# Block 1's layer norm statistics ahead of the last two angle tables, and the loads of x for blocks 2 and 3 behind block 0's state DMAs

## The chip, the cores and the metric

The kernel runs on one core of a Trainium2 chip. The metric is the device time of one execution in microseconds (us), the median of several runs. One further execution is taken by the hardware profiler; the times of single instructions come from that one.

The engines have these names in the profile: PE is TensorE, PEld its weight loads, DVE is VectorE, ACT is ScalarE, POOL is GpSimd, and SP is SyncE, which here only issues DMAs. DMAs issued by SP and ACT run on queue q1, those issued by POOL on queue q0.

## The reference

The input x has 2048 tokens of 512 channels. It is normalized (mean and variance per token, no gain), and the result xn goes through two branches that are added to x.

```python
xn = _layernorm(x)
# branch A: a diagonal state space layer
Lam_bar = exp(dt * Lam)                       # 512 complex poles
Bu = einsum("bld,pd->blp", xn, B_bar)
h  = Lam_bar * h + Bu[:, t]                   # over 2048 tokens
yA = 2 * einsum("blp,dp->bld", h, C).real + xn * Dskip
# branch B: a gated feed-forward layer, 512 -> 1792 -> 512
yB = (silu(xn @ w1) * (xn @ w3)) @ w2
out = x + yA + yB
```

## The kernel before

**Blocks.** The tokens are worked on in four blocks of 512 (blocks 0 to 3), each of four chunks of 128 tokens. `glu(b)` makes the two products with w1 and w3 of block b in 14 steps f (L587 matmuls, `gu_ps` in PSUM); ScalarE takes them out as g and u (L596, L597), and VectorE multiplies a pair of steps (L604) into the tile `act`. `bu(b)` makes the products with B (L454), which ScalarE copies to u (L456). The tile `act` of a block collects gates and states, and `y_fast(n)` multiplies half a block (pair n, 256 tokens) by w2 and C in one go.

**The states.** A complex recurrence is turned into a real one by rotating with tables of cosine and sine (`tabe`): `table_angles(pt, n)` makes the angles on VectorE (L376 to L380) for n of the four groups of 128 poles, and ScalarE makes cosine and sine of them (L384). Then VectorE rotates (`pre_a`, L484 and others), scans along the tokens (L505) and rotates back (`post_a`, `post_b`). `post_c` adds the second half of the rotation to `act` with an accumulating DMA from POOL (L527). For block 0 there are two of these, the state DMAs of the change's title.

**Layer norm.** For block 0 it is done first. For block 1, `ln_tasks_vector(1)` gives two lists: `ln1a` has four statistics (L219 and L220, one for each chunk) and the reciprocal root on POOL (L254, L255); `ln1b` has four normalizations (L224), each with a DMA transpose from SP (L247). For blocks 2 and 3 ScalarE does it (L274, L280, L290).

**Pair products.** `y_fast(n)` uses seven products of quarter matrices instead of eight, with sums of the operands made beforehand. For pair 0 their order is 1, 5, 2, 6, 4, 3, 7. The sums of rows s3 and s2 of pair 0 (L1000) are written into the tiles of x of block 0 and block 1, whose content is no longer needed by then. The last reader of these tiles is `res_list(b)`: it multiplies xn by Dskip on VectorE (L933) and adds x with an accumulating DMA from POOL (L937), the residual DMA. The sum s1 is made by another accumulating DMA (L1007). A third sum, s4, is made on VectorE after product 2 (L1096) and is the left operand of product 3.

**What sets the order.** Every engine and every queue works in the order in which the program issues. The order on VectorE comes from `bg`, a list of background tasks with costs: `bg.add(cost, fn)` puts a task at the end of the list, and the loops of matmuls call `bg.fill()`, which takes tasks from the front as long as the estimated time of VectorE is not ahead of that of TensorE. A task may also issue DMAs. The order on SP is that of the issues: weights, x of block 1, the transposed B and C, the four transposes of block 1, then `late_loads` (w2, Dskip, x of block 2 in four loads and x of block 3 in one, L162), and then nothing before the transposes of block 2.

The tasks concerned are put into the list here:

```python
bg.add(3.6, lambda: table_angles(2, 2))
for t in ln1a:
    bg.add(*t)
for t in ln1b:
    bg.add(*t, ("ln", 1))
bg.add(0.0, late_loads, ("ln", 1))
```

Of the kernel before, what the change touches and what calls it, by code (L numbers as in the profile page):

```python
# [63 lines left out]
def kernel(  # L64
# [17 lines left out]
    nc = tc.nc  # L82
# [67 lines left out]
    x_all = xpool.tile([P, NBLK, CPB, D], BF16, name="x_blk")  # L150
# [8 lines left out]
    def load_x(b, parts=1):  # L159
        n = CPB // parts  # L160
        for i in range(0, CPB, n):
            nc.sync.dma_start(out=x_blk[b][:, i:i + n, :], in_=xv[:, b * CPB + i:b * CPB + i + n, :])  # L162
# [19 lines left out]
    def late_loads():  # L182
        nc.sync.dma_start(out=w2_sb, in_=B_w2.rearrange("(t p) d -> p t d", p=P))
        nc.sync.dma_start(out=dskip_row, in_=A_Dskip.partition_broadcast(P))
        load_x(2, 4)
        load_x(3)

# [23 lines left out]
    bg = Filler(LEAD)  # L211
# [37 lines left out]
    def ln_tasks_vector(b):  # L249
        csl = slice(b * CPB, (b + 1) * CPB)  # L250

        def finish_stats():
            vpe = lnp.tile([P, CPB], FP32, name="vpe")
            nc.gpsimd.tensor_scalar(out=vpe, in0=mv_all[:, csl, 1], scalar1=LN_EPS, scalar2=None, op0=ALU.add)  # L254
            nc.gpsimd.tensor_tensor(out=rstd_all[:, csl], in0=vpe, in1=mhalf, op=ALU.pow)  # L255

        def apply(cl):
            if cl == 0:
                ln_alloc(b)
            ln_apply(b, cl)  # L260
            ln_transpose(b, cl)

        first = [(0.85, lambda cl=cl: ln_stats(b, cl)) for cl in range(CPB)] + [(0.0, finish_stats)]
        second = [(0.4, lambda cl=cl: apply(cl)) for cl in range(CPB)]
        return first, second
# [74 lines left out]
    def sin_step(until=None):  # L340
        while sins and (until is None or until not in sins_done):
            key, fn = sins.popleft()
            fn()
            sins_done.add(key)
            if until is None:
                break
# [23 lines left out]
    def table_angles(pt, n=1):  # L370
        if pt + n > 3:
            sin_step((pt + n - 4, 0))
        slots = scratch[:, 0:2 * NPT * 2 * TBLK].bitcast(FP32).rearrange("p (h i t) -> p h i t", h=2, t=TBLK)
        ang, rnd = slots[:, 0, pt:pt + n, :], slots[:, 1, pt:pt + n, :]
        for i in range(n):
            nc.vector.tensor_scalar(out=ang[:, i, :], in0=iota_f, scalar1=turn[:, pt + i:pt + i + 1], scalar2=None,  # L376
                                    op0=ALU.mult)
        nc.vector.tensor_scalar(out=rnd, in0=ang, scalar1=MAGIC, scalar2=None, op0=ALU.add)
        nc.vector.scalar_tensor_tensor(out=ang, in0=rnd, scalar=MAGIC, in1=ang, op0=ALU.subtract, op1=ALU.subtract)
        nc.vector.tensor_scalar(out=rnd.bitcast(DT.int32), in0=ang.bitcast(DT.int32), scalar1=0x7FFFFFFF, scalar2=None,  # L380
                                op0=ALU.bitwise_and)
        for k in range(pt, pt + n):
            for i, (src, bias, scale) in enumerate(((rnd, halfpi, -TWO_PI), (ang, 0.0, -TWO_PI))):
                sins.append(((k, i), lambda k=k, i=i, src=src[:, k - pt, :], bias=bias, scale=scale: nc.scalar.activation(  # L384
                    out=tabe[:, k, i, :], in_=src, func=ACT.Sin, bias=bias, scale=scale)))
# [76 lines left out]
    def ssm_tasks(b, posts_last=False, between=(), middle=(), late=()):  # L462
# [76 lines left out]
        def add(*fns):  # L539
            for fn in fns:  # L540
                bg.add(0.0 if fn in transfers else 1.2 if fn in scans0 or fn in scans1 else 1.16, fn,
                       ("scan", b) if fn in scans0 else ("post", b) if fn in post0 else ("ssm", b))

        if b == 0:
            add(*pre0, *scans0, *post0, *pre1, *scans1, *post1)
            return
        add(*pre0)
        for t in middle:
# [32 lines left out]
    def glu(b):  # L581
# [76 lines left out]
        for f in range(f0, NFT):  # L658
            if f == AHEAD[b]:
                if b == 0:  # L660
                    ssm_tasks(0)
                if b == 2:
                    sin_step(("squares", 3, CPB - 1))
                    bg.flush(("bu", 0))
                    steps.extend(bu_fast(b, 0))
                    second = lambda: bu_fast(b, 1)
                else:
                    bu(b)
# [497 lines left out]

    ln_alloc(0)
    ln1a, ln1b = ln_tasks_vector(1)
    bg.add(3.6, lambda: table_angles(2, 2))
    for t in ln1a:  # L1170
        bg.add(*t)
    for t in ln1b:
        bg.add(*t, ("ln", 1))
    bg.add(0.0, late_loads, ("ln", 1))
    bg.add(0.2, params_w)
    gate = glu(0)
# [33 lines left out]
    def keep_ends(b):  # L1210
# [3 lines left out]
        nc.vector.tensor_copy(out=ends, in_=act(b)[:, CPB - 1].rearrange("p (h k) t -> p h k t", h=2)[:, :, NFH:NK, P - 1])  # L1214

    ssm_tasks(1, between=[(0.2, lambda: keep_ends(0))])
    gate = glu(1)
    gate()
# [6 lines left out]
    for cl, o in held:  # L1225
        nc.sync.dma_start(out=ov[:, cl, :], in_=o)
    bg.add(*difference(1))
    ssm_tasks(2, between=res_list(3), late=[(0.2, lambda: keep_ends(1)), *row_sums(2, *pairs[2]), *column_sums(3)])
    bg.first(bu_sums(2))
    gate = glu(2)  # L1230
# [52 lines left out]
```

## Time and profile before

| | |
|---|---|
| median of 3 runs | 200.94 us (200.86 to 201.03) |
| profiled execution, from its first to its last instruction (span) | 199.5 us |
| what lies around the span (median less span) | 1.44 us |
| busy: PE | 195.6 us (98%) |
| busy: DVE | 181.8 us (91%) |
| busy: ACT | 135.0 us (68%) |
| busy: POOL | 51.5 us (26%) |
| mean granted TensorE clock | 0.999 |
| moved by DMA | 25.12 MB, mean 126 GB/s |

The page names only the span of the profiled execution; its own device time is not given beside it, so the 1.44 us are the difference to the median. All times in what follows are microseconds from the start of the span. A timeline row gives start, length, engine, line, operation and tiles, then in brackets the idle time of the engine ahead of it and what ended it. A row of the windows gives the stretch, its length, then the busy time and the number of instructions of PE, PEld, DVE, ACT and POOL, the granted clock, the mean busy share of the 16 DMA engines, and GB/s. A queue's row gives packets, MB and the time of its packets as a share of 16 engines. A row of a DMA issue gives the count, the size and the time from issue to landing.

### The profile page before, as it was taken

The page shows a single profiled execution, that of the slowest core. Times are in us where ns is not written, and L with a number is a line of the kernel's source. Part 1 is how long each engine was busy: PE and PEld are TensorE (multiplying, and loading weights), DVE is VectorE, ACT ScalarE, POOL GpSimd, SP SyncE. Part 2 cuts the span into 40 slices and gives each one's busy share as a digit, 9 for nine tenths or more (in the row PEclk, how much of TensorE's full clock was granted, in tenths as well). Part 3 has the DMA queues.
Part 4 walks back from the last instruction along what each step waited for, and adds up shares of the span by engine and source line. Part 5 has one row for each costly group of instructions (what it writes and reads, how often), then busy time and mean ns, then how long its engine had stood idle before and what let it go on. Part 6 is the DMA issues. An engine that isn't in the chain of part 4 may idle for free.

```text
span 199.5 us, 3700 instructions
## 1 busy us (share of the span) xinstructions
PE 195.6 (98%) x1401; PEld 130.7 (65%) x1401; DVE 181.8 (91%) x254; ACT 135.0 (68%) x281; POOL 51.5 (26%) x75
## 2 busy tenths in 40 slices
PE   8999999999999999999999999999999999999994
PEld 2774444444444488866555468888566678888893
DVE  3689699999999999989999997999999999999972
ACT  4699897699999996968998684362588783111220
POOL 7180289700411134041202305040021303310000
PEclk9999999999999999999999999999999999999999
DMA  4999996991497054730997455838137732941111
GB/s 138 326 277 200 302 186 124 343 273 23 69 181 141 0 105 82 135 105 0 156 148 119 89 92 98 172 83 132 53 59 129 149 56 52 174 92 36 53 44 40
DMA packets 32258, 25.12 MB, mean 126 GB/s; under 512 B 16240, under 2 KB 29936, under 8 KB 32240
## 3 DMA queue, kind: packets, MB, share of 16 engines
q0 software_dynamic: 6128, 11.38, 33.5%
q1 hardware_dynamic: 25536, 13.21, 26.8%
q10 hardware_dynamic: 576, 0.30, 0.5%
q8 instruction: 11, 0.18, 0.4%
q14 instruction: 7, 0.06, 0.1%
HBM read 7.74 MB, written 2.10 MB: 49 GB/s over the span
## 4 chain that ended last, share of the span: by engine, by line
PE 95%; DMA 2%; SPq 1%; issue 0%; DVE 0%
PE gu_ps L587 34%; PE gu_ps L1054 17%; PE y_ps L1054 10%; PE gu_ps L848 7%; PE bu_ps L1054 7%; PE bu_ps L454 3%; PE y_ps L454 3%; PE y_ps L869 3%; PE y_ps L780 3%; DMA w_sb<-in_B_w_dram 2%; PE gu_ps L619 2%; PE gu_ps L780 2%; PE bu_ps L869 1%; PE bu_ps L780 1%; PE bu_ps L619 1%; SPq L166 0%
## 5 line engine op out<-in xcount | busy, mean ns | idle before, releaser
L587 PE MATMUL gu_ps<-xnT,w_sb 128*128 128x512 bf16 x312 | 69.6, 379 | 0.0
L587 PEld LDWEIGHTS <-w_sb 128*128 128x128 bf16 x312 | 30.5, 98 | 34.2
L1054 PEld LDWEIGHTS <-act 128*128 128x128 f16 x462 | 43.5, 98 | 5.4
L596 ACT ACTIVATE g<-gu_ps 128x512 bf16<-128x512 f32 x41 | 24.8, 606 | 6.0 <-PE gu_ps L587 3.6
L597 ACT ACTIVATE u<-gu_ps 128x512 bf16<-128x512 f32 x41 | 24.8, 606 | 4.5 <-PE gu_ps L587 3.7
L505 DVE TENSOR_TENSOR_SCAN u<-rho,ends,u 128x512 bf16<-128x512 f32 x16 | 20.0, 1270 | 0.0
L527 POOL DMA_DIRECT2D act<-p x7 | 9.2, 1320 | 34.0 <-DVE act L519 22.1
L1054 PE MATMUL gu_ps<-w_sb,act 128*128 128x256 bf16 (+3 forms) x126 | 16.0, 267 | 0.0
L848 PE MATMUL gu_ps<-xnT,w_sb 128*128 128x512 bf16 x64 | 15.9, 379 | 0.0
L604 DVE TENSOR_TENSOR act<-g,u 128x1024 f16<-128x1024 bf16 x21 | 14.2, 679 | 0.4 <-ACT u L597 0.4
L860 ACT ACTIVATE g<-gu_ps 128x512 bf16<-128x512 f32 x14 | 8.4, 599 | 5.4 <-PE gu_ps L848 5.0
L454 PEld LDWEIGHTS <-bt 128*128 128x128 bf16 x64 | 6.3, 98 | 7.5
L1077 ACT ACTIVATE x_blk<-gu_ps 128x256 f32<-128x256 f32 (+1 forms) x9 | 3.3, 368 | 10.6 <-PE gu_ps L1054 10.6
L1054 PE MATMUL bu_ps<-w_sb,act 128*128 128x256 bf16 (+3 forms) x84 | 10.4, 264 | 0.0
L1054 PE MATMUL gu_ps<-ct,act 128*128 128x256 f16 (+1 forms) x72 | 10.4, 267 | 0.0
L848 PEld LDWEIGHTS <-w_sb 128*128 128x128 bf16 x64 | 6.3, 98 | 4.8
L505 DVE TENSOR_TENSOR_SCAN u<-rho,u 128x512 bf16<-128x512 f32 x8 | 9.2, 1206 | 0.0
L1054 PEld LDWEIGHTS <-x_blk 128*128 128x128 f16 x88 | 8.6, 98 | 1.0
L1054 PEld LDWEIGHTS <-tw 128*128 128x128 f16 x88 | 8.6, 98 | 1.0
L513 DVE TENSOR_TENSOR p<-u,tabe 128x2048 f16<-128x2048 bf16 (+1 forms) x8 | 8.7, 1085 | 0.1
L519 DVE TENSOR_TENSOR act<-u,tabe 128x2048 f16<-128x2048 bf16 (+1 forms) x8 | 8.7, 1083 | 0.0
L488 DVE TENSOR_TENSOR u<-u,tabe 128x2048 bf16<-128x2048 bf16 x7 | 8.5, 1219 | 0.1
(203 smaller groups left out, 392.5 us busy)
## 6 DMA issues: line engine op xcount, KB each, us to landing
act<-p POOLq DMA_DIRECT2D x6, 512.0 KB, 6.1
xn<-x_blk POOLq DMA_DIRECT2D x4, 512.0 KB, 5.5
out_dram<-xn SPq DMA_DIRECT2D x15, 128.0 KB, 1.7
w_sb<-in_B_w_dram SPq DMA_DIRECT2D x1, 1792.0 KB, 8.2
act<-act POOLq DMA_DIRECT2D x5, 352.0 KB, 4.6
w_sb<-in_B_w_dram SPq DMA_DIRECT2D x2, 768.0 KB, 6.4
u<-p POOLq DMA_DIRECT2D x3, 512.0 KB, 5.1
w_sb<-in_B_w_dram SPq DMA_DIRECT2D x4, 256.0 KB, 4.9
```

What stands on the lines that cost most here:

```text
L454: nc.tensor.matmul(out=ps, lhsT=bt[:, ri, dt, pt * P:(pt + 1) * P], rhs=xnT_blk[b][:, dt, :], start=(dt == 0), stop=(dt == NDT - 1))
L505: nc.vector.tensor_tensor_scan(out=v, data0=rho[:, pt:pt + 1].to_broadcast([P, TBLK]), data1=v, initial=init, op0=ALU.mult, op1=ALU.add)
L513: nc.vector.tensor_tensor(out=by_state(st["p16"][:, csl]), in0=by_chunk(st["g"][:, :, ::-1, tsl]), in1=by_chunk(tabe[:, psl, 2:0:-1, tsl]) ...
L519: nc.vector.tensor_tensor(out=by_state(act_state(b, hf)[:, csl]), in0=by_chunk(st["g"][:, :, :, tsl]), in1=by_chunk(tabe[:, psl, 0:1, tsl] ...
L527: gp.dma_start(out=a, in_=p16, accum_op=ALU.add)
L587: nc.tensor.matmul(out=ps[:, tsl], lhsT=w[:, dt, f * P:(f + 1) * P], rhs=xnT[:, dt, tsl], start=(dt == 0), stop=(dt == NDT - 1))
L596: nc.scalar.activation(out=g16[:, f % 2, :], in_=g_ps, func=ACT.Silu)
L597: nc.scalar.activation(out=u16[:, f % 2, :], in_=u_ps, func=ACT.Copy)
L604: nc.vector.tensor_tensor(out=act_gates(b, f - 1), in0=split(g16), in1=split(u16), op=ALU.mult)
L780: nc.tensor.matmul(out=out[:, h * TH:(h + 1) * TH], lhsT=left[:, h, k, :], rhs=right[:, k, :], start=(start and h == 0 and k == 0), stop=( ...
L848: nc.tensor.matmul(out=ps, lhsT=w[:, dt, f * P:(f + 1) * P], rhs=xnT[:, dt, :], start=(dt == 0), stop=(dt == NDT - 1))
L1054: nc.tensor.matmul(out=out, lhsT=left[:, k, :], rhs=right[k][:, cols], start=(start and k == 0), stop=(k == NK - 1), skip_group_check=True)
```

## The change

It has two parts. The four statistics of block 1 and the reciprocal root (`ln1a`) are put into the task list ahead of the angles of the last two pole groups (`table_angles(2, 2)`), not behind them. And the loads of x of blocks 2 and 3 leave `late_loads` for a task of their own, which comes behind all tasks of block 0's states. The task begins with a memset on POOL of two elements per partition, one in the first chunk of each of the two blocks; the load of the first chunk of block 2 must wait for it, and on SP the other four loads stand behind that one.

```diff
@@ -182,6 +182,9 @@
     def late_loads():
         nc.sync.dma_start(out=w2_sb, in_=B_w2.rearrange("(t p) d -> p t d", p=P))
         nc.sync.dma_start(out=dskip_row, in_=A_Dskip.partition_broadcast(P))
+
+    def last_x_loads():
+        nc.gpsimd.memset(x_all[:, 2:4, 0, 0:1], 0.0)
         load_x(2, 4)
         load_x(3)
 
@@ -543,6 +546,7 @@
 
         if b == 0:
             add(*pre0, *scans0, *post0, *pre1, *scans1, *post1)
+            bg.add(0.0, last_x_loads)
             return
         add(*pre0)
         for t in middle:
@@ -1166,9 +1170,9 @@
 
     ln_alloc(0)
     ln1a, ln1b = ln_tasks_vector(1)
-    bg.add(3.6, lambda: table_angles(2, 2))
     for t in ln1a:
         bg.add(*t)
+    bg.add(3.6, lambda: table_angles(2, 2))
     for t in ln1b:
         bg.add(*t, ("ln", 1))
     bg.add(0.0, late_loads, ("ln", 1))
```

In the order of the instructions of the two kernels this is what differs. VectorE has the four statistics ahead of the second gate product, which is followed by the five instructions of the angles; all else on it is in the same order. POOL has the memset between the second state DMA of block 0 and the residual DMA of block 0. On SP and ScalarE the order is the same; the first of the five loads, and the first reader of block 2's x on ScalarE (L274), also wait for POOL. TensorE's order is the same.

## The prediction

> **What bounds the kernel now.** I read the busy time of the engines by stage first, to see whether any time is there to be won.
>
> ```profile
> 7.16:13.00 5.84, 5.84 (x98) 5.56 (x99) 3.83 (x8) 4.55 (x12) 3.25 (x8) 1.00 1.24 323
> 13.00:100.00 87.00, 87.00 (x495) 48.16 (x493) 82.97 (x114) 76.76 (x158) 29.04 (x38) 1.00 0.68 144
> 100.00:196.80 96.80, 96.78 (x783) 74.52 (x780) 90.84 (x123) 49.78 (x104) 15.49 (x16) 1.00 0.52 94
> ```
>
> The second number of a row is the stage's length, the third the busy time of TensorE. From 7.16 us to 196.8 us TensorE lacks 0.02 us in all, at a granted clock of 1.00. So the chain that ended last is TensorE's matmuls, one behind the other. The change touches nothing before 14.68 us (the first moved VectorE instruction) and not the last stores, so almost nothing can be won; what counts is whether TensorE is made to wait. If it is, the wait goes into the time in full, as nothing later can catch up.
>
> Next, VectorE around the place where the gated loads will now run. Columns: start, length, line, operation.
>
> ```profile
> 58.49 1.08 DVE L977 TENSOR_TENSOR tw<-w_sb,tw 128x1792 f16<-128x1792 bf16 x1
> 59.50 0.88 DVE L1000 TENSOR_TENSOR x_blk<-act 128x1408 f16<-128x1408 f16 x1
> ...
> 63.29 0.88 DVE L1000 TENSOR_TENSOR x_blk<-x_blk,act 128x1408 f16<-128x1408 f16 x1
> ...
> 73.77 0.88 DVE L1096 TENSOR_TENSOR act<-act,x_blk 128x1408 f16<-128x1408 f16 x1
> ```
>
> VectorE runs these without idle time; its first pause after them is 0.36 us at 78.53. The two subtractions of L1000 overwrite the x tiles of blocks 0 and 1, so they wait for the residual DMAs of L937, which read those tiles. From the DMA issues of two windows, with the time to landing last:
>
> ```profile
> xn<-x_blk POOLq DMA_DIRECT2D x1, 512.0 KB, 6.9
> ```
> ```profile
> xn<-x_blk POOLq DMA_DIRECT2D x1, 512.0 KB, 5.1
> ```
>
> Issued at 52.08 and 57.67, they land at 58.98 and 62.77: only 0.52 us ahead of each subtraction (59.50, 63.29). These are the two thin places. The third is TensorE's own. L1096 makes s4, the left operand of the third product of the first pair, and ends at 73.77 + 0.88 = 74.65. On the chain that product is the next piece on bu_ps:
>
> ```profile
> 73.62 2.40 PE y_ps L1054 x22
> 76.03 1.20 PE bu_ps L1054 x11
> ```
>
> The timeline has its first matmul start at 75.86, its weight load 0.10 us ahead of that, at 75.76. So VectorE may be 75.76 - 74.65 = 1.1 us late there before TensorE stops.
>
> **Part one: statistics ahead of the angle tables.** Same instructions in another order. Four statistics at 0.82 us each (L219 starts at 19.57 and 20.39) take 14.68 to 17.95; a gate product of 0.57 follows; the angles' 3.5 us (14.68 to 18.18 before) end at 22.0. Block 1's x, issued at 6.05 and 7.7 on its way, is there at 13.75, so the earlier statistics do not wait. GpSimd's reciprocal root (22.15 to 23.5 before) now runs under the angles and VectorE's 1.47 us wait at 23.54 goes. What is late next: L484 at 26.02 needs ScalarE's u copy, which ends at 25.17 + 0.60 = 25.77, so of the 1.5 us some 0.15 us is kept and the rest becomes a new wait there. The angles, 3.8 us later, are read by a sine at 25.66, 3.6 us of cover left. The transposes of block 1 stand on SP behind those of C (until 26.17), so they do not come earlier. On the path: nothing; VectorE leads by 0.15 us from 26 us on.
>
> **Part two: the gated loads.** The memset stands on GpSimd behind the second state DMA (50.95) and ahead of the residual DMA (52.08). It needs no other engine. Small operations on GpSimd took 0.10 us when alone (L208) and up to 1.26 us beside VectorE (L357). I take 0.2, as the loads' start is all it moves: the residual DMA behind it could be issued 1.1 us late and would still find the state DMA's data moving (until about 56.0 us). SP, which issued the five loads at 33.47 to 36.54, stands still from there to about 52.3 and issues them to 55.4. Behind them on SP is only the transpose at 77.05, so nobody else waits.
>
> Taken away: 1 MB beside the first state DMA, which took 9.1 us against the second's 5.5. It lands at 46.66, and its reader (L513, 47.69) did not wait: worth nothing.
>
> Added: 1 MB into 53.6 to 61 us (the weight load of 31.88 shows its first bytes at about 33, 1.3 us on; hence 52.3 + 1.3). There the residual DMAs have the engines to themselves: share 1.07 from 52.5 to 58.5, 0.18 to 59.0, 0.91 to 62. At 358 GB/s (mean of 34.5 to 38 us, loads alone) 1 MB takes 2.9 us. The trace has no load arriving while accumulating DMAs wait, so the question is who goes first. The nearest row is the first state DMA, issued at 37.56 behind queued loads:
>
> ```profile
> q1 hardware_dynamic: 683, 0.63, 99.7%
> ```
> ```profile
> q0 software_dynamic: 277, 0.28, 65.4%
> q1 hardware_dynamic: 499, 0.48, 52.1%
> ```
>
> From 39.3 to 41.5 us the accumulating queue q0 moves nothing; only from 41.5 to 44.2, as the loads end, does it get its 0.28 MB. Whoever was queued first was served first. A row against it: from 98.5 to 102 us both ran at once, q0 with 440 packets and transposes on q1 with 389, one for one; but transposes are not loads.
>
> [...]
>
> Served by order (the value I take, as its row is about plain loads): the second state DMA and the first residual DMA are ahead; the loads run from 58.5, when that one's data end, for 2.9 us to 61.4; the second residual DMA, whose data began at 59.0, begins 2.4 us later and lands at 62.77 + 2.4 - 0.15 = 65.0. L1000 starts there and not at 63.29: 1.75 us late with the landing's signal. No VectorE pause stands between it and L1096, so s4 is 1.75 us late, and TensorE stops for 1.75 - 1.1 = 0.65 us. The first x chunk lands at about 59.5, against 61.92 when ScalarE reads it (L274). The gate at 64.69 ends at 65.37 and frees a tile that ScalarE takes at 68.33: 2.96 us of cover. s1's DMA (60.67 + 3.8 = 64.5) is needed at 71.22. None of these falls.
>
> Sum: span 199.5 + 0.65, with the 1.44 us that lies between the profiled span and the 200.94 median: 201.6 us. Bounds of this term: 0.3 us (loads at 380 GB/s, half a microsecond of idle engine used) to 1.0 us, thus 201.3 to 202.0.
>
> [...]
>
> **Rivals.** *Loads first.* If the loads pass both residual DMAs, as they passed q0 at 39.3 us, the first lands at 58.98 + 2.9 - 0.15 = 61.7, L1000 starts 2.3 us late, TensorE stops for 1.2 us: 202.15. For it: residual and loads come within half a microsecond of each other (52.1 on GpSimd, 52.3 on SP). Against: the state DMA is certainly ahead.
>
> *In turns, not slower.* If the queues alternate, a 1 KB load packet of 46 ns follows each accumulating one. By the second state DMA's rate (512 packets in 3.7 us on 16 engines, 0.115 us each) some 23 of its 32 packets per engine and then 8 of 4 KB are stretched by 46 ns: 31 x 0.046 = 1.4 us, up to 1.9 us if the idle tenths inside the transfers are lost too. The first residual DMA lands at 60.3 to 60.8, L1000 is 0.8 to 1.3 us late, TensorE stops for 0 to 0.2 us: 201.0. It decides at 1.1 us of lateness. For it: the row at 98.5 us. Then the change does nothing that shows.
>
> *Faster.* It would need pauses of TensorE, of which there are 0.02 us; only scatter of the start gives it.
>
> **How the numbers follow.** 0.2% is 0.4 us, about what a measurement of this kernel can tell from no change: above 201.34 is slower. Served by order 0.42, loads first 0.23, in turns 0.30, other mishaps 0.03 (a late x chunk stopping ScalarE), faster 0.02. Of the forecast's own range 0.04 lies under 201.34. So slower 0.42 - 0.04 + 0.23 + 0.03 = 0.64, same 0.34, faster 0.02. The range reaches from the turns case with no stop (200.85) to loads first with its bound (202.4); its likeliest case alone has 201.3 to 202.0.
>
> **What would show it.** Right: no wait on VectorE at 23.5 us and a new one of about 1.3 us ahead of L484; a wait ahead of the second L1000 at about 63 us, put down to the DMA xn or x_blk; a TensorE pause of 0.65 us ahead of the third product at 76 us, and none elsewhere. The wait ahead of the first L1000, at 59.5 us, means loads first; both waits under 1.1 us together mean turns. Wrong in kind: a pause of TensorE before 70 us, or a ScalarE wait ahead of L274, or a time under 200.5.

## The result and the profile after

The changed kernel takes 203.0 us (median of 6 runs, 202.81 to 205.17), the kernel before 200.9 us (6 runs, 200.75 to 201.86). The ratio is 1.0113 with a 95% interval of 1.0081 to 1.0145: slower by 2.1 us, where the forecast was 0.66 us. The direction was right, the time lies above the range.

The profiled execution is the longest of the six, 205.17 us with a span of 203.3; the other five have spans of 201.0 to 201.3 and times of 202.81 to 203.05. It holds an event of its own, which the clock row of the page shows as the one digit below 9:

```profile
span 203.3 us, 3704 instructions
...
PEclk9999999999999996999999999999999999999999
```

So two things have to be told apart: the 2.1 us that all executions have, and some 2 us that one of six has on top. First TensorE by stage, from the windows (columns as before):

```profile
13.00:60.00 47.00, 47.00 (x220) 21.32 (x218) 44.06 (x58) 42.45 (x80) 13.80 (x26) 1.00 0.81 170
60.00:80.00 20.00, 18.04 (x113) 11.23 (x112) 17.25 (x25) 16.29 (x40) 5.90 (x7) 0.95 0.50 110
80.00:100.00 20.00, 20.00 (x145) 14.36 (x144) 18.05 (x28) 14.36 (x34) 4.24 (x6) 0.96 0.46 86
100.00:200.50 100.50, 100.50 (x803) 76.56 (x801) 94.61 (x128) 53.42 (x110) 15.99 (x17) 1.00 0.55 97
```

From 13 us on TensorE has a pause in one stage only. Between 60 and 80 us it lacks 20.00 - 18.04 = 1.96 us, and in this row and the next the granted clock is below 1. VectorE's timeline shows what led up to it:

```profile
60.38 0.89 DVE L1004 TENSOR_TENSOR x_blk<-act 128x1408 f16<-128x1408 f16 x1 [1.01 <-DMA xn<-x_blk]
...
66.53 0.89 DVE L1004 TENSOR_TENSOR x_blk<-x_blk,act 128x1408 f16<-128x1408 f16 x1 [2.28 <-DMA xn<-x_blk]
...
77.02 0.88 DVE L1100 TENSOR_TENSOR act<-act,x_blk 128x1408 f16<-128x1408 f16 x1
```

Lines of the changed kernel stand 3 or 4 further down: L1004 is the L1000 of before, L1100 is L1096, L1058 is L1054, L487 is L484. Both subtractions now wait for a residual DMA (the bracket names its tiles, xn and x_blk): 1.01 + 2.28 = 3.29 us. Nothing behind them has slack on VectorE, so s4 ends at 77.02 + 0.88 = 77.90, and 77.90 - 74.65 = 3.25 us later than before. TensorE's timeline has the other end of this wait:

```profile
74.64 1.36 PE L1058 MATMUL y_ps<-tw,act 128*128 128x256 f16 x11
77.96 1.50 PE L1058 MATMUL bu_ps<-w_sb,act 128*128 128x256 bf16 x7 [1.96 <-DVE act L1100]
...
82.04 0.93 PE L1058 MATMUL gu_ps<-w_sb,act 128*128 128x256 bf16 x7
```

The same two products in the kernel before:

```profile
74.66 1.36 PE L1054 MATMUL y_ps<-tw,act 128*128 128x256 f16 x11
75.86 0.93 PE L1054 MATMUL bu_ps<-w_sb,act 128*128 128x256 bf16 x7
```

The third product starts at 77.96, against 75.86 before: 2.1 us later. That is the lateness less the slack, 3.25 - 1.1 = 2.15, and it is the whole of the measured 2.1 us. (The bracket's 1.96 us count from the end of the product ahead, 1.36 us behind its start. Undisturbed, the next one begins 1.20 us behind that start, as the rows of before show, so what is lost is 0.16 us more than the bracket says: 2.12 us.) The rows of the changed kernel also show the event of this one execution: seven matmuls take 1.50 us where the same seven take 0.93 at 82.04. That was the clock, as narrower windows show:

```profile
74.77:78.18 3.41, 1.45 (x14) 1.07 (x12) 3.41 (x7) 0.18 (x1) 2.98 (x3) 1.00 0.81 154
78.18:81.60 3.42, 3.42 (x19) 2.43 (x18) 3.22 (x6) 3.01 (x5) 0.93 (x1) 0.50 0.62 116
81.60:85.00 3.40, 3.40 (x33) 3.04 (x32) 2.69 (x3) 1.56 (x6) 0.00 (x0) 1.00 1.12 129
```

For 3.4 us, from 78.18 to 81.60, the granted clock is 0.50; half of that, 1.7 us, is lost: 199.5 + 2.1 + 1.7 = 203.3, the span of this execution.

Why the residual DMAs are late can be seen in the DMA queues of three windows (packets, MB, share of 16 engines; q0 has the accumulating DMAs that POOL issues, q1 what SP issues, the loads among it; the few DMAs of ACT are not on q1 but on q10: 432 packets, 0.26 MB up to 7 us before). From 57 to 59 us, while the first residual DMA runs:

```profile
q0 software_dynamic: 71, 0.29, 90.3%
q1 hardware_dynamic: 72, 0.07, 13.3%
```

From 59.5 to 61.5 us, after its data are through and with the second residual DMA already issued (57.45):

```profile
q1 hardware_dynamic: 701, 0.67, 100.1%
q0 software_dynamic: 16, 0.00, 0.5%
```

So while the first residual DMA ran, it shared the engines with the loads, one packet each (71 against 72). (In their first microsecond, from 54.5 to 55.5 us beside the second state DMA, the loads got less: 28 packets against 125.) But in between the two residual DMAs the loads had the engines to themselves, for 2.0 us (701 packets against 16). The DMA issues of the two residual DMAs, in two windows:

```profile
xn<-x_blk POOLq DMA_DIRECT2D x1, 512.0 KB, 8.5
```
```profile
xn<-x_blk POOLq DMA_DIRECT2D x1, 512.0 KB, 9.0
```

Issued at 51.86 and 57.45, they land at 60.35 and 66.41. Before they took 6.9 and 5.1 us and landed at 58.98 and 62.77: the first is 1.4 us late, the second 3.6 us. In windows of 0.1 us the 3.6 us fall into three parts. The data of the first residual DMA end at about 59.4 and not at 58.4: 1.0 us. Between its data and those of the second lie about 2.25 us (until 61.65), filled by loads, where 0.65 us lay before (until 59.05): 1.6 us. And from its first data to its landing the second takes 4.8 us and not 3.7: 1.0 us. From 62 to 64 us 41 load packets still come between its own; whether they are all of this last microsecond is not shown.

### The profile page after: what moved, and what is told of

It is laid out like the page before. It is cut to its first block, busy times and chain, and to the rows that moved or that the text cites. A ratio compares the mean times of both kernels' runs of the same rounds, so it can differ in the third digit from the quotient of the medians.

```text
span 203.3 us, 3704 instructions
## 1 busy us (share of the span) xinstructions
PE 197.6 (97%) x1401; PEld 132.0 (65%) x1401; DVE 181.9 (89%) x254; ACT 134.9 (66%) x281; POOL 46.8 (23%) x76
## 4 chain that ended last, share of the span: by engine, by line
PE 69%; DVE 17%; DMA 7%; issue 4%; SPq 1%; ACT 0%; POOL 0%; POOLq 0%; DVEq 0%
PE gu_ps L1058 17%; PE gu_ps L591 16%; PE y_ps L1058 8%; PE gu_ps L852 7%; PE bu_ps L1058 6%; DMA xn<-x_blk 4%; DVE u L508 4%; PE y_ps L873 3%; PE y_ps L784 3%; DVE act L608 3%; DVE u L491 2%; DVE p L487 2%; DMA w_sb<-in_B_w_dram 2%; PE gu_ps L623 2%; PE gu_ps L784 2%
## 5 line engine op out<-in xcount | busy, mean ns | idle before, releaser
L1058 PEld LDWEIGHTS <-act 128*128 128x128 f16 x462 | 43.9, 99 | 8.0 <-DVE act L1100 2.2
L1058 PE MATMUL gu_ps<-w_sb,act 128*128 128x256 bf16 (+3 forms) x126 | 15.9, 267 | 0.0
L1058 PE MATMUL bu_ps<-w_sb,act 128*128 128x256 bf16 (+3 forms) x84 | 11.0, 273 | 2.0 <-DVE act L1100 2.0
L1058 PE MATMUL gu_ps<-ct,act 128*128 128x256 f16 (+1 forms) x72 | 10.4, 267 | 0.0
L1058 PEld LDWEIGHTS <-x_blk 128*128 128x128 f16 x88 | 9.0, 103 | 1.5
L1058 PEld LDWEIGHTS <-tw 128*128 128x128 f16 x88 | 8.6, 98 | 1.0
L487 DVE TENSOR_TENSOR p<-u,tabe 128x2048 bf16<-128x2048 bf16 x6 | 7.3, 1221 | 1.5 <-ACT u L459 1.5
```

Source lines behind the costliest of these rows:

```text
L487: nc.vector.tensor_tensor(out=st["p"][:, :, ::-1, :], in0=st["g"], in1=tabe[:, psl, 2:0:-1, :], op=ALU.mult)
L1058: nc.tensor.matmul(out=out, lhsT=left[:, k, :], rhs=right[k][:, cols], start=(start and k == 0), stop=(k == NK - 1), skip_group_check=True)
```

## Experiments

Theory A: the second part does it all, through the residual DMAs: late landing, late L1004, late s4, and TensorE pays what exceeds about 1.1 us. Its rivals put the loss on the memset's stay on POOL or beside VectorE, on the moved statistics, or on having loads gated at all. All comparisons are with the kernel before, on the same chip.

### One part at a time

**e1_stats_only** keeps the first part alone: of the two parts of the diff, `last_x_loads` is undone.

> Part one alone: the statistics of block 1 ahead of the last two angle tables, the loads of x where they were. Theory A (the loss is the gated loads, which take turns with and then overtake the residual DMAs, so that the two subtractions of the row sums wait on VectorE, s4 is 3.2 us late and TensorE stops for 2.1 us): 200.9 us, ratio 1.000, no wait ahead of either subtraction, no TensorE pause. Theory B (the new order of VectorE costs something itself, through a gate product or a sine that comes later): 201.3 us or more, with a wait on ScalarE or TensorE between 14 and 30 us.

201.04 us against 201.07, ratio 0.9992 (0.9976 to 1.0009). The first part costs and brings nothing.

**e2_gate_only** keeps the second part alone: `ln1a` stays behind `table_angles(2, 2)`.

> Part two alone: the loads of x of blocks 2 and 3 gated, VectorE's old order. Theory A: the whole loss, 203.0 us (202.8 to 203.2), with waits of about 1.0 and 2.3 us ahead of the two subtractions. Theory B: less than the whole, under 202.5 us.

203.3 us against 201.07, ratio 1.0109 (1.0077 to 1.0142): all of the loss, and a little above the expected 202.8 to 203.2. VectorE's and TensorE's timelines show the same three waits:

```profile
60.16 0.89 DVE L1004 TENSOR_TENSOR x_blk<-act 128x1408 f16<-128x1408 f16 x1 [1.03 <-DMA xn<-x_blk]
66.19 0.89 DVE L1004 TENSOR_TENSOR x_blk<-x_blk,act 128x1408 f16<-128x1408 f16 x1 [2.15 <-DMA xn<-x_blk]
```
```profile
77.61 0.94 PE L1058 MATMUL bu_ps<-w_sb,act 128*128 128x256 bf16 x7 [2.03 <-DVE act L1100]
```

The pause is 2.03 us and the seven matmuls behind it take 0.94 us: here the clock stayed at full speed, the span is 201.3 us and the time of this execution 203.19. The clock event is therefore no part of the 2.1 us.

**e3_memset_only** keeps the memset at its place on POOL, but lets it write a tile of its own, so no load waits for it; the five loads go back into `late_loads`:

```diff
-
-    def last_x_loads():
-        nc.gpsimd.memset(x_all[:, 2:4, 0, 0:1], 0.0)
         load_x(2, 4)
         load_x(3)
+
+    def last_x_loads():
+        nc.gpsimd.memset(idle_pair, 0.0)
...
```

> Both parts, but the memset writes a small tile of its own, so that it stands on GpSimd at the same place and the loads do not wait for it. Theory A: 200.9 us, as the loads run at 33 us again. Theory C (the memset beside VectorE holds up the residual DMA's issue on GpSimd): the first residual DMA lands after 60 us and the time is over 202 us.

201.07 us, ratio 1.0002 (0.9986 to 1.0017). The residual DMAs land at 59.06 and 62.76, as before. The memset is harmless; it is the loads.

**e4_gate_first_state** keeps gate and loads, but puts the gate behind the first state DMA, 13 us earlier:

```diff
-            add(*pre0, *scans0, *post0, *pre1, *scans1, *post1)
+            add(*pre0, *scans0, *post0)
             bg.add(0.0, last_x_loads)
+            add(*pre1, *scans1, *post1)
```

> Both parts, but the gate stands behind block 0's first state DMA (37 us) and not behind the second (51 us): the same wait on SP for the same memset, the loads at some 39 to 45 us where VectorE waits for no DMA that shares the engines with them. Theory A: 200.9 us (200.7 to 201.2), no wait ahead of the subtractions. Theory D (a gated load is costly wherever it stands, through SP's standstill or the memset): over 202 us.

201.03 us, ratio 0.9996 (0.9983 to 1.0009). The five loads are issued from 39.05 to 42.35 and all have landed at 46.8; the residual DMAs land at 59.05 and 62.62. A gate as such costs nothing. What costs is the place in which the loads then run.

### How much of the megabyte

**e5_only_x3** gates only the single 512 KB load of block 3, **e6_only_x2** only the four 128 KB loads of block 2; the others stay in `late_loads`.

The edit of e5 (that of e6 is its counterpart):

```diff
+        load_x(2, 4)
 
     def last_x_loads():
-        nc.gpsimd.memset(x_all[:, 2:4, 0, 0:1], 0.0)
-        load_x(2, 4)
+        nc.gpsimd.memset(x_all[:, 3:4, 0, 0:1], 0.0)
         load_x(3)
```

> Only the load of block 3's x (one DMA of 512 KB) is gated; block 2's four loads stay at 33 us. Half the bytes. Theory A: the first residual DMA lands 0.5 to 1.2 us later than before, the second 1.5 to 2 us later (all gated bytes, 1.5 us of them, go ahead of it); s4 is 1.0 to 1.6 us late, TensorE stops for 0 to 0.5 us: 200.9 to 201.4 us. Theory E (the delay does not go by bytes but by the number of queues that alternate): nearly the whole loss, over 202.5 us.

> Only the four loads of block 2's x (128 KB each) are gated; block 3's load stays early. Half the bytes, in four issues. Theory A: as for block 3 alone, 200.9 to 201.4 us. Theory E: over 202.5 us. Whoever issues four DMAs on SP takes longer for it, so the bytes may come later and the second residual DMA may be hit more than the first.

| gated | residual DMAs land | from issue to landing | waits ahead of L1004 | time, against before | ratio |
|---|---|---|---|---|---|
| none (before) | 58.98, 62.77 | 6.9, 5.1 | 0, 0 | | |
| block 3 (e5) | 60.61, 63.66 | 9.0, 6.5 | 1.52, 0 | 201.77, 201.0 | 1.0038 (1.0022 to 1.0053) |
| block 2 (e6) | 59.61, 63.93 | 8.1, 6.9 | 0.66, 0.54 | 201.16, 201.0 | 1.0008 (0.9992 to 1.0023) |
| both (the change) | 60.35, 66.41 | 8.5, 9.0 | 1.01, 2.28 | 203.0, 200.9 | 1.0113 (1.0081 to 1.0145) |

The profiled executions do not run in step: the second state DMA, which both parts of the change leave alone, is issued between 49.98 (e8) and 51.03 us (e10). So the times from issue to landing compare better than the landings.

The waits nearly add up (1.52 + 1.20 = 2.72, against 3.29), the times do not (0.77 + 0.16 = 0.93, against 2.1): the first microsecond or so of lateness is free, whoever brings it. Theory E falls, as both are far under 202.5 us.

e5 costs more than the expected 200.9 to 201.4 us: a miss. The 0.06 us that its s4 at 75.81, 1.16 us later than before, would leave behind a slack of 1.1 us is the wrong sum, because this execution runs ahead of that of the kernel before. In its own time the second product starts at 74.39, so the third could have started 1.20 us later, at 75.59; it starts at 75.86, 0.27 us late:

```profile
74.39 1.36 PE L1058 MATMUL y_ps<-tw,act 128*128 128x256 f16 x11
75.86 0.94 PE L1058 MATMUL bu_ps<-w_sb,act 128*128 128x256 bf16 x7
```

Reckoned in this way the loss is 2.12 us in the changed kernel and 2.19 us in e2. The median of e5 is 0.77 us above the kernel before. Its profiled execution (201.5 us) is one of the faster of ten (201.17 to 202.42), and what the slower ones lose, and where, is not shown.

The same reckoning ties the time to this one place. In all fourteen profiles the span ends 123.6 to 123.9 us behind the start of the third product (in that of the changed kernel once the 1.7 us of half clock are taken off), so what moves this start moves the time by as much.

### The same load behind the residual DMAs

**e7_gate_after_residuals** puts the gate behind `res_tasks(1)`, that is behind both residual DMAs. **e10_x3_after_residuals** leaves block 2's loads where the change has them and puts only block 3's there.

The edit of e7:

```diff
-            bg.add(0.0, last_x_loads)
...
     res_tasks(1)
+    bg.add(0.0, last_x_loads)
     ln_alloc(2)
```

> Both parts, but the gate stands behind both residual DMAs (58 us). Theory A: the first subtraction does not wait; the second residual DMA shares the engines with the loads and may still be 1 us late. A new wait instead: ScalarE reads block 2's x from 62 us on, and its first chunk lands at 62 to 64 us, so ScalarE waits 0.5 to 2 us ahead of the row sums of x, and TensorE stops for what the free PSUM tiles do not cover: 201 to 202.5 us.

> The whole change, with block 3's load taken to a gate of its own behind both residual DMAs (58 us; it is read at 80 us), block 2's four loads behind the state DMAs as in the change. Theory A: as with block 2's loads alone, both subtractions wait some 0.6 us each, s4 is 1.1 us late at the most, TensorE stops for 0.2 us at the most: 200.9 to 201.3 us. If the number of gated DMAs counts and not what runs ahead of the second residual DMA: over 202.5 us.

e7: 201.49 us, ratio 1.0027 (1.0003 to 1.0051). The subtractions do not wait, so the mechanism of the change is gone, but x of block 2 now comes too late for its reader on ScalarE:

```profile
63.16 0.63 ACT L277 ACTIVATE xn<-x_blk 128x512 bf16<-128x512 bf16 x1 [1.22 <-DMA x_blk<-in_A_x_dram]
```

That profiled execution (201.33 us) has no pause on TensorE behind 13 us, while the ten executions range from 200.73 to 203.01. Where the slower ones lose is left open. The second residual DMA is not held up here: it lands 5.3 us after its issue (5.1 before). The loads are issued from 58.39 on, but from 58.4 to 61.6 us, until its data are through, the queues have no row of q1 at all:

```profile
q0 software_dynamic: 127, 0.52, 95.7%
```

e10: 201.88 us, ratio 1.0032 (1.0017 to 1.0046), where 200.9 to 201.3 was expected: a miss. Block 3's load is issued at 58.75, behind the second residual DMA, and still loads run beside that one. From 61 to 63 us:

```profile
q0 software_dynamic: 88, 0.36, 96.5%
q1 hardware_dynamic: 85, 0.09, 15.8%
```

The residual DMAs land at 60.43 and 65.16, the waits are 0.79 and 0.95 us, and TensorE pauses 0.42 us ahead of the third product (76.72), which is 0.58 us late in its own time. So here being issued behind an accumulating DMA was not enough to put a load behind it (85 load packets against its 88). In e7, where no other load was under way, the loads did stay behind (no packet of q1 until 61.6 us); in e10 block 2's loads were already moving. Whether that is the reason is not tested.

### Who goes first

**e11_x2_one_load** loads block 2 in one DMA of 512 KB, so that both loads are issued from 51.53 to 52.8 us, ahead of the first residual DMA's data.

```diff
-        load_x(2, 4)
+        load_x(2)
         load_x(3)
```

> The whole change, with block 2's x in one load of 512 KB and not four, so that SP has issued all gated bytes within 1 us. Theory F (a new accumulating DMA starts on an engine only when the loads queued there have drained; one that already runs takes turns with them): the first residual DMA, issued at about the same time, starts behind all of the 1 MB and lands at 61.3 to 62.3 us, the second follows it at its own pace and lands at 64.8 to 65.8; the first subtraction waits 2 to 3 us, the second under 0.5 us; s4 is 2.3 to 3 us late, 202.1 to 202.9 us. Theory G (the queues take turns throughout): the first lands before 60.8 and the second before 64.8 us, and the time is under 201.8 us.

202.99 us, ratio 1.0093 (1.0067 to 1.0119). The loads land at 57.98 and 62.89, the residual DMAs at 60.71 and 65.06, the waits are 2.00 and 0.57 us. Theory G falls (under 201.8 us). The numbers of theory F nearly come out (202.1 to 202.9 us, waits of 2 to 3 us and under 0.5 us), but its mechanism does not hold as stated: the first residual DMA does not wait for all queued loads, it takes turns with the second load. The queues from 58 to 60 us, with the first residual DMA running, and from 60 to 61 us, ahead of the second:

```profile
q0 software_dynamic: 88, 0.35, 88.1%
q1 hardware_dynamic: 91, 0.09, 16.6%
```
```profile
q1 hardware_dynamic: 332, 0.34, 96.4%
...
q0 software_dynamic: 14, 0.00, 0.8%
```

It is the pattern of the changed kernel again: one for one beside the running accumulating DMA (91 packets against 88), loads alone at the boundary to the next (332 against 14). With two large loads the boundary ahead of the first residual DMA is filled as well (363 packets of q1 against 10 of q0 from 56 to 57 us), so part of the lateness moves from the second wait to the first. The median stays at that of the change; the sum of the waits (2.57 us) belongs to the profiled execution, the fastest of the four (202.27 us, the others 202.91 to 203.1). Why the next accumulating DMA moved next to nothing at the boundary (0.00 MB in both rows) until the queued loads were nearly through is not settled by these runs.

### The path from the late landing to the time

**e8_sums_later** keeps the whole change and puts other VectorE work ahead of the subtractions, so that they come when the data are there:

```diff
     first_sums = row_sums(0, *pairs[0])
-    for t in first_sums[:2]:
-        bg.add(*t)
     for fn in finish_c[2:]:
         bg.add(1.4, fn, "tw")
+    for t in first_sums[:2]:
+        bg.add(*t)
     bg.add(*difference(0))
-    bg.add(*first_sums[2])
     for i, which in ((1, 2), (1, 0), (1, 1), (1, 3)):
         weight_sum(i, which)
+    bg.add(*first_sums[2])
```

> The whole change with the contention left as it is, but VectorE's first subtraction of pair 0 is put behind the four weight operations of 2.7 us and the second behind the four sums of weights of 2.7 us, so that VectorE works while the residual DMAs are late. Theory A: both waits go (under 0.3 us together), s4 is in time, no TensorE pause at the third product: 200.9 to 201.2 us. If the loss came by another way than the late subtractions (s1's DMA, a gate product, a clock): still over 202 us.

200.96 us against 201.0, ratio 1.0000 (0.9987 to 1.0012): the loss is gone. The second residual DMA lands at 65.46, 2.7 us later than before and 8.8 us after its issue (5.1 before), but the timeline has neither subtraction waiting:

```profile
61.49 0.89 DVE L1004 TENSOR_TENSOR x_blk<-act 128x1408 f16<-128x1408 f16 x1
...
65.89 0.88 DVE L1004 TENSOR_TENSOR x_blk<-x_blk,act 128x1408 f16<-128x1408 f16 x1
...
73.11 0.89 DVE L1100 TENSOR_TENSOR act<-act,x_blk 128x1408 f16<-128x1408 f16 x1
```

The rest of VectorE's work filled the time, and s4 is done at 74.00. So the loss came through VectorE's idle time ahead of s4; of another way nothing is left that these runs can tell (the interval reaches to 0.12%, 0.24 us).

**e12_three_ops_more** makes s4 as late without any DMA: the kernel before, with one weight sum of 128x1792 (about 1.1 us) written three more times ahead of the second subtraction.

```diff
+        def again():
+            bg.add(0.0, lambda: nc.vector.tensor_tensor(out=t2[0], in0=t1[0], in1=b22[0], op=ALU.subtract), "tw")
...
+    for _ in range(3):
+        weight_sum.again()
     bg.add(*difference(0))
```

> The kernel before, with the lateness made without any DMA: VectorE computes one of the weight sums (L977, 128x1792, 1.12 us from one to the next) three times more ahead of the second subtraction. The loads stay at 33 us. Theory A (all that counts of the contention is how late s4 is; 1.1 us of it are free, the rest stops TensorE): s4 is 3.2 to 3.4 us late, TensorE stops for 2.1 to 2.3 us ahead of the third product, 203.0 to 203.2 us, as much as the change costs. If the late DMAs cost something besides (s1, the x tiles, ScalarE's reads): less than that, under 202.6 us.

203.35 us against 201.08, ratio 1.0138 (1.0092 to 1.0184); 2.27 us, a little above expectation. VectorE, then TensorE:

```profile
62.76 3.34 DVE L981 TENSOR_TENSOR tw<-w_sb 128x1792 f16<-128x1792 f16 x3
...
66.35 0.89 DVE L1004 TENSOR_TENSOR x_blk<-x_blk,act 128x1408 f16<-128x1408 f16 x1
```
```profile
77.78 0.94 PE L1058 MATMUL bu_ps<-w_sb,act 128*128 128x256 bf16 x7 [1.95 <-DVE act L1100]
```

No DMA is late here (the residual DMAs land at 58.99 and 62.67), s4 ends at 77.72, and TensorE pauses 1.95 us, against 1.96 in the changed kernel. It is the lateness that counts, whatever makes it.

**e9_change_again** is the changed kernel once more, for the size and the clock event.

> The changed kernel once more, unchanged, on the same chip as the next two. Most executions 202.8 to 203.3 us. If an execution lies over 204.5 us, its clock should be below 1 for some 3.4 us behind the pause of TensorE at 76 us, as in the profiled execution of the first measurement; with a clock of 1.00 throughout it should be near 203.0 us.

202.94 us, ratio 1.0098 (1.0078 to 1.0119), waits of 0.95 and 2.10 us, a pause of 1.71 us, the clock at 1.00, and no execution of four above 203.2. The loss repeats (1.9 us here); the half clock does not, so what was expected of it stays untested.

No version here is faster than the kernel before. e1, e3, e4, e6 and e8 equal it, which fits a TensorE that had no time to give.

## Why the prediction was right and wrong

**What bounds the kernel: right.** TensorE had nothing to win, and its one new pause behind 13 us, ahead of the third product, went into the time in full.

**Part one: right.** VectorE's wait at 23.5 us is gone and another stands ahead of L487; 1.3 us was forecast:

```profile
25.77 1.23 DVE L487 TENSOR_TENSOR p<-u,tabe 128x2048 bf16<-128x2048 bf16 x1 [1.46 <-ACT u L459]
```

e1 confirms that this is worth nothing.

**The gate itself: right in effect, off in three sizes.** The memset took 0.62 us beside VectorE, not 0.2, and e3 shows that it does not matter. The issue of the five loads on SP took from 52.16 to 57.1 us, not to 55.4: the slowest took about 1.3 us each while the accumulating DMAs ran. And the first load packet moved at 54.6 us, 2.4 us after the first issue, where the forecast took 1.3 us (53.6). Both put more of the loads beside and between the two residual DMAs.

**The slack of 1.1 us: right.** 3.25 us of lateness gave 2.1 us, e12's 3.07 us gave 2.27, e6's waits of 1.2 us nothing that shows. The forecast reckoned as if every execution ran in step with the profiled one. e5 and e10, near the edge, cost 0.8 us each by their medians; their profiled executions show 0.27 and 0.58 us of it at the third product, the rest is open.

**The term that failed: "served by order".** It had the first residual DMA untouched and the second landing at 65.0, for 1.75 us of lateness and a stop of 0.65 us. The runs show 60.35 (1.4 us late) and 66.41, 3.25 us of lateness and a third product 2.1 us late. The error lies in this: the forecast took one of two rows as the rule and kept the other as a rival, though the changed kernel shows both kinds of behaviour, each in its own situation. The row of 39.3 us has an accumulating DMA that had not begun; there the loads went alone (683 packets, none of q0). The row of 98.5 us has one that ran; there the queues took turns (440 packets against 389). In the changed kernel the loads meet both in succession (701 against 16, 72 against 71), so the costs had to be added and not weighed against each other. The forecast moved the second residual DMA's first data by 2.4 us, to 61.4; the measured 61.65 is close to it, but by other terms, 1.0 us for the slower first residual DMA and 1.6 us of loads alone. From there the forecast let it run at its old pace, and it took 1.0 us longer.

**The rivals.** "In turns" had the first landing right (60.3 to 60.8), but not its parts: it put 23 x 0.046 = 1.06 us on the state DMA, which took only 0.4 us longer (5.9 us against 5.5). It had no account of what the loads do ahead of the second. "Loads first" had passing loads, but ahead of the first. Its price for the sum, one load time of 2.9 us less 0.15 and less the slack, came nearer (202.15) than the forecast, by chance. Of the signs that the forecast named, a wait ahead of the first subtraction was to mean loads first, and two waits under 1.1 us together turns; there were waits ahead of both, 3.29 us together. For the two landings no case had the true pair. The upper bound of 202.4 was that of loads first, in which 1 MB delays the path by its own transfer time of 2.9 us at the most. The measured 3.25 us is above that, as the loads cost twice: alone between the two residual DMAs, and in turns beside both.

**The clock: not in the forecast.** Its sum takes the clock as 1.00, as the stage rows of before have it. In the profiled execution the clock halved (0.50), for one stretch of 3.42 us, after one of 3.41 us with a pause of 1.96 us, in which TensorE was busy 1.45 us. Of the 18 executions of the four kernels whose profile has a pause of about 2 us (the change, e2, e9, e12) two show the longer time, 205.17 and 205.0, both with a mean clock of 0.992; no other execution on record is below 0.998. What makes the clock halve behind one such pause and not behind another (1.00 in e2, after 2.03 us) is not shown.

**The queues.** Where the first residual DMA ran, the two queues took turns by packets (71 against 72). At the boundary (16 against 701) it is open whether the next accumulating DMA's packets already stood ready, as no row shows that. When the stretch began, at 59.4 us, its issue lay 2.0 us back; in the kernel before its first data came 1.4 us after its issue.

## What to carry to other kernels

Before moving a load to a "free" stretch of the DMA engines, list the transfers that run there, and find for each the compute instruction that waits for it and its lead: here 0.52 us of lead on a tile to be overwritten, and 1.1 us of slack behind it had to pay for 1 MB. Two rows of a trace that seem to contradict each other are worth a second look for what differs between them; both may apply, one after the other. If a transfer must stay late, putting other work of the waiting engine ahead of the wait may take the loss back; here it took back all of it (e8).

## What the hardware showed that was not expected

- Plain loads on q1 alternated packet for packet with a running accumulating DMA on q0 (72 packets against 71 from 57 to 59 us, 91 against 88 in e11; in their first microsecond it was 28 against 125), but went alone at the boundary between two of these: 701 packets against 16 from 59.5 to 61.5 us, 332 against 14 in e11. The second of two accumulating DMAs thereby landed 3.6 us later, for 1 MB of loads that take an estimated 2.9 us alone (at the 358 GB/s of 34.5 to 38 us before). Loads beside the second residual DMA were seen even with one issued behind it (e10); in e7, with no load under way, the loads moved no packet until its data were through.
- A pause of TensorE of 1.96 us was followed, in one execution of six, by 3.42 us at half clock (0.50; 1.7 us lost); pauses of 2.03 and 1.71 us in e2 and e9 left the clock at 1.00.
- Issuing a load on SP took up to 1.3 us while accumulating DMAs ran, and the five of them 4.97 us, against 3.1 us before. The first load packet moved 2.4 us after the issue, and 3.3 us in e7 (58.39 to 61.7), against 1.2 us for the weight load of 31.88 before.
